# Smaller squares and stores in layer one, another schedule of weight decoding, and another buffer layout in layer two

## The chip, the cores and the metric

The kernel runs on one NeuronCore of a Trainium2 chip. Its five engines have queues of their own: PE multiplies matrices, DVE, ACT and POOL work on elements, and SP issues nearly all DMAs (transfers by the core's 16 DMA engines). The number compared is the device time of one execution in microseconds (us), the median of several.

## The reference

Float32 throughout, with 4 x 576 = 2304 tokens in 512 columns:

```python
x = attention(q, k, v, f)          # causal, with a decay per key; (4, 8, 576, 64) -> (2304, 512)
h = x @ moe_w_in                   # 512 x 2048
y = (h - np.tanh(h)) @ moe_w_out   # 2048 x 512
h = y @ moe2_w_in                  # layer one, below
r = np.maximum(h, 0.0)
out = (r * r) @ moe2_w_out         # layer two, below
```

## The kernel before

**Arithmetic.** Every float32 operand of a matmul is split into two parts, `hi` (written by ACT) and `lo` (the rest, by a subtraction on DVE), and a product is the sum of three matmul passes. The last two matrix products, here **layer one** and **layer two**, use Strassen and Winograd's scheme besides: a 2 x 2 block product is made of seven products instead of eight, numbered 1 to 7, from sums and differences of blocks.

**Stages.** Attention and the first MLP run first and interleaved, up to some 660 us. Then layer one: three blocks `i` of 768 tokens by eight column pairs `p` of the weights make 24 units `u`. A unit has seven products (`l1_product`) of six matmuls (128x128 weights, 384 tokens). The first four (6, 1, 7, 5) stand in the unit's own step, the others (2, 4, 3) in the next unit's, interleaved. `after1` evacuates each from PSUM: the sums go through `u2` into the four quarters of the unit's result, relu is taken on ACT, the square on POOL (`store1`), and SP stores the result to `gscr` in DRAM. Layer two has 36 groups `n` of seven products. `g_load` brings a group's four quarters from `gscr` into a buffer `graw` (SP), `g_sums` forms the differences (DVE), `g_split` makes the two parts in `gc` (ACT, then DVE), `l2_product` runs the matmuls, and `after2` and `store2` write the output.

**Weights.** `decode_w` turns the words of a weight matrix into float32: ACT (L193, L194), DVE (L200, L202), then the differences `wsum` on POOL (L246). Phase 1 are the eight column pairs of layer one: here (1,7) is the decode of pair 7. They are split at once (`split_all`, L302 and L303) into `ws` and `wq`. Phase 2 are the eight blocks of layer two; (2,k) is the decode of block k. These go to DRAM (`wscr`, L252 to L256), and `final_load` and `final_split` fetch and split them when layer one has done with the room. All decodes share two buffers "wide" (`wfull`, `wsum`), and one runs at a time: a decode asked for while another is at work waits in `pending` until `decoded()` is called. That happens in phase 1 behind the last split, and in phase 2 when the store of the sums has been issued. The words of block k + 1 are asked for (`load_w`) inside the decode of block k, and all the `wraw` of phase 2 share one buffer. A phase 2 decode is asked for at the start of unit 5 and of every second one behind it (`PRE`); phase 1 decodes come from `feed`, one per unit.

**Order.** A small clock in the code places the work: `cw.step` is one product, and `cw.later(k, fn)` runs `fn` k steps on. What is called in this sequence has its priority from it; a list scheduler then sets the order on each engine, and pools of buffers by `tag` set what must wait for what. `tc.high_priority` moves a piece of the program ahead in that ranking.

Of the kernel before, what the change touches and what calls it, by code (L numbers as in the profile page):

```python
# [10 lines left out]
F32 = mybir.dt.float32  # L11
# [9 lines left out]
P = 128  # L21
# [88 lines left out]
def fused_kernel(ctx: ExitStack, tc: tile.TileContext, q, k, v, f, w1i, w1o, w2i, w2o, out):  # L110
# [1057 lines left out]
    def after1(u, k, t):  # L1168
        i, p = units1[u]
        t3 = blocks3(t)  # L1170

        def add(o, a, b):
            nc.vector.tensor_tensor(o, in0=a, in1=b, op=ALU.add)  # L1173

        if k == 6:
# [5 lines left out]
        elif k == 1:  # L1181
            add(u2[u], t, u2[u])
        elif k == 7:
            gf[u, 1] = box2["m2"].tile([P, 3, 2, P], F32, tag="gt", name=f"g1_{u}", bufs=2)
            add(gf[u, 1][:, :, 1], t3, blocks3(u2[u]))
        elif k == 5:
            add(gf[u, 1][:, :, 1], t3, gf[u, 1][:, :, 1])
        elif k == 2:
            gf[u, 0] = m1.tile([P, 3, 2, P], F32, tag="x", name=f"g0_{u}", bufs=2)
            nc.scalar.activation(gf[u, 0][:, :, 0], t3, AF.Relu)  # L1190
        elif k == 4:
            g = gf[u, 1]
            add(g[:, :, 0], t3, blocks3(u2[u]))
            nc.scalar.activation(g, g, AF.Relu)  # L1194
            cw.later(1, lambda: store1(u, 1))
        else:
            g = gf[u, 0]
            add(g[:, :, 1], t3, blocks3(u2[u]))
            nc.scalar.activation(g[:, :, 1], g[:, :, 1], AF.Relu)
            cw.later(1, lambda: store1(u, 0))  # L1200

    def store1(u, fi):
        i, p = units1[u]
        g = gf.pop((u, fi))
# [260 lines left out]
```

## Time and profile before

| | us |
|---|---|
| median of three runs (lowest, highest) | 1063.67 (1059.83, 1066.32) |
| the profiled execution's own time | 1064.87 |
| its span in the profile | 1063.2 |

Times of the profile below count from the start of the span. The time of the execution is 1.7 us longer than the span, and 1.2 us above the median. TensorE's mean granted clock was 0.989 of its full speed. All engines have idle time, but PE little. What the page calls the idle time before an instruction, and names after an arrow, is the event that came last before it.

### The profile page before, as it was taken

What the parts mean: (1) busy time and instruction counts of PE and PEld (TensorE: products, weight loads), DVE (VectorE), ACT (ScalarE), POOL (GpSimd) and SP (SyncE); (2) the same over time, 40 slices, a digit from 0 to 9 for tenths busy, and PEclk for the clock granted to TensorE, in tenths of its full rate; (3) what the DMA queues carried; (4) which work ended last, traced back from release to release, by engine and by line L of the source; (5) the groups of instructions that cost most, each with busy time, mean ns of one, the idle gap of its engine ahead of it and who ended that gap; (6) DMA issues with size and microseconds to landing.
All of it is one profiled execution on the core that took longest, in us unless ns stands there. A gap on an engine that the chain in (4) does not pass through costs nothing.

```text
span 1063.2 us, 20566 instructions
## 1 busy us (share of the span) xinstructions
PE 1010.9 (95%) x7246; PEld 961.1 (90%) x7246; DVE 757.1 (71%) x1597; ACT 585.7 (55%) x1177; POOL 435.6 (41%) x576
## 2 busy tenths in 40 slices
PE   7989999999999999999999999988889869999998
PEld 5778899999999999999998878988888869999998
DVE  5897954777777767777756786577667788777775
ACT  5887854566766756766643574445355453333332
POOL 4663632455445555455502332666756340000000
PEclk9998999999999999999999999999999989999999
DMA  8937642333433333432231234657668853444442
GB/s 226 278 125 229 205 126 74 88 94 86 110 98 86 94 96 86 119 88 63 70 92 56 84 119 139 213 168 248 212 232 266 264 159 111 129 120 122 132 124 80
DMA packets 191335, 146.47 MB, mean 138 GB/s; under 512 B 83616, under 2 KB 168928, under 8 KB 191232
## 3 DMA queue, kind: packets, MB, share of 16 engines
q1 hardware_dynamic: 191184, 145.12, 46.1%
q8 instruction: 57, 0.93, 0.4%
q14 instruction: 46, 0.38, 0.1%
q10 hardware_dynamic: 48, 0.03, 0.0%
HBM read 100.47 MB, written 39.92 MB: 132 GB/s over the span
## 4 chain that ended last, share of the span: by engine, by line
PE 59%; DMA 7%; DVE 7%; issue 4%; POOL 4%; ACT 3%; SPq 2%; DVEq 0%; ACTq 0%; POOLq 0%
PE y L993 15%; PE h L953 15%; PE o L1302 13%; PE pt L737 4%; PE pv L808 3%; PE r L1161 3%; DMA wscr<-wfull 2%; POOL g L1205 2%; PE s L699 2%; PE s L700 2%; DVE gc L1289 1%; POOL wsum L246 1%; DMA gscr<-g 1%; DVE wfull L202 1%; DMA graw<-gscr 1%
## 5 line engine op out<-in xcount | busy, mean ns | idle before, releaser
L993 PE MATMUL y<-ghl,w 128*128 128x256 f32 (+1 forms) x1536 | 247.9, 304 | 2.9 <-DVE ghl L974 2.3
L993 PEld LDWEIGHTS y<-ghl,w 128*128 128x128 f32 x1536 | 211.5, 191 | 15.8 <-DVE ghl L974 3.6
L953 PE MATMUL h<-x,w 128*128 128x256 f32 x1344 | 199.6, 290 | 4.9 <-POOL w L218 3.8
L953 PEld LDWEIGHTS h<-x,w 128*128 128x128 f32 x1344 | 174.4, 190 | 9.7 <-POOL w L218 5.0
L1288 ACT ACTIVATE gc<-graw 128x1792 fp32r<-128x1792 f32 x36 | 60.6, 1699 | 112.9 <-DVE graw L1279 92.7
L1302 PE MATMUL o<-ws,gc 128*128 128x256 f32 x864 | 117.9, 287 | 0.0
L1161 PE MATMUL r<-yt,ws 128*128 128x384 f32 x576 | 109.5, 337 | 6.7 <-DVE g L1173 6.5
L1302 PEld LDWEIGHTS o<-ws,gc 128*128 128x128 f32 x864 | 111.2, 195 | 0.0
L1161 PEld LDWEIGHTS r<-yt,ws 128*128 128x128 f32 x576 | 99.8, 188 | 10.6 <-DVE g L1173 8.0
L530 POOL TENSOR_SCALAR Pb<-neg,ccol 128x384 f32<-128x384 f32 (+2 forms) x96 | 69.0, 718 | 91.4 <-PE pt L737 73.9
L644 ACT ACTIVATE Pb<-Pb,st 128x384 f32<-128x384 f32 (+2 forms) x96 | 67.6, 704 | 68.1 <-DVE st L635 67.8
L1302 PE MATMUL o<-wq,gc 128*128 128x256 f32 x648 | 92.8, 287 | 11.5 <-ACT gc L1288 7.3
L1205 POOL TENSOR_TENSOR g<-g 128x768 f32<-128x768 f32 x48 | 81.1, 1704 | 48.1 <-ACT g L1194 38.7
L658 POOL TENSOR_SCALAR Pb<-Pb,st 128x384 f32<-128x384 f32 (+2 forms) x96 | 67.0, 698 | 81.7 <-DVE st L654 50.9
L1302 PEld LDWEIGHTS o<-wq,gc 128*128 128x128 f32 x648 | 85.0, 194 | 12.8 <-ACT gc L1288 7.6
L1161 PE MATMUL r<-yt,wq 128*128 128x384 f32 x432 | 84.6, 337 | 11.5 <-ACT g L1190 6.2
L1161 PEld LDWEIGHTS r<-yt,wq 128*128 128x128 f32 x432 | 75.2, 188 | 14.8 <-ACT g L1190 7.5
L1289 DVE TENSOR_TENSOR gc<-graw,gc 128x1792 fp32r<-128x1792 f32 x36 | 73.2, 2054 | 15.8 <-ACT gc L1288 15.8
L635 DVE CUSTOM_DVE_ANT_0 Pb<-s,Pb 64x288 f32<-64x288 f32 (+2 forms) x160 | 73.8, 476 | 13.2 <-PE s L700 7.3
L966 DVE TENSOR_TENSOR g<-h,g 128x512 f32<-128x512 f32 x72 | 49.5, 687 | 31.1 <-ACT g L963 29.9
L246 POOL TENSOR_TENSOR wsum<-wfull 128x256 f32<-128x256 f32 x32 | 28.2, 882 | 84.1 <-DVE wfull L202 72.4
L743 DVE TENSOR_TENSOR PT<-pt,PT 128x384 fp32r<-128x384 f32 (+2 forms) x96 | 55.1, 574 | 10.3 <-ACT PT L742 5.6
(152 smaller groups left out, 1898.7 us busy)
## 6 DMA issues: line engine op xcount, KB each, us to landing
gscr<-g SPq DMA_DIRECT2D x48, 384.0 KB, 3.2
graw<-gscr SPq DMA_DIRECT2D x144, 128.0 KB, 2.6
wraw<-in_moe_w_in_dram SPq DMA_DIRECT2D x32, 512.0 KB, 4.7
wraw<-in_moe_w_out_dram SPq DMA_DIRECT2D x32, 512.0 KB, 5.3
neg<-cscr SPq DMA_DIRECT2D x32, 288.0 KB, 3.6
qk<-in_k_dram SPq DMA_DIRECT2D x48, 128.0 KB, 2.7
v<-in_v_dram SPq DMA_DIRECT2D x48, 128.0 KB, 2.7
wst<-wscr SPq DMA_DIRECT2D x6, 896.0 KB, 5.9
```

What stands on the lines that cost most here:

```text
L530: nc.gpsimd.tensor_scalar(pb[:rows, o : o + w], t[:rows, :w], ccol[:rows, ti, b * H + h : b * H + h + 1], 1.0, op0=ALU.add, op1=ALU.mult)
L635: nc.vector.tensor_tensor_reduce(out=d, in0=t[:rows, src : src + m], in1=d, scale=-0.125, scalar=3.0e38 if j == 0 else stat(0, x)[:rows], ...
L644: nc.scalar.activation(d, d, AF.Exp, bias=stat(len(parts) - 1, x)[:rows], scale=-1.0, accum_out=stat(2, x)[:rows])
L658: nc.gpsimd.tensor_scalar(d, d, r, 1.0, op0=ALU.mult, op1=ALU.mult)
L743: cw.later(LAG['trlo'], lambda: nc.vector.tensor_tensor(dst[1], src, dst[0].bitcast(F32), op=ALU.subtract))
L953: nc.tensor.matmul(o, lhsT=win(fc, wh, dc), rhs=xpart(j, dc, xh), start=dc == 0 and wh + xh == 0, stop=dc == ND - 1 and wh == 1)
L993: nc.tensor.matmul(o, lhsT=wout(fc, wh, i * P, P), rhs=ghl[:, xh, fj * n : fj * n + n], start=s == 0 and fj == 0 and wh + xh == 0 and i % ...
L1161: nc.tensor.matmul(t, lhsT=wprod(1, p, k, wh)[:, dc * P : (dc + 1) * P], rhs=yt[i, k][:, xh, dc], start=k in FIRST and dc == 0 and wh + xh ...
L1205: nc.gpsimd.tensor_tensor(g, in0=g, in1=g, op=ALU.mult)
L1288: nc.scalar.activation(c[:, 0], t[:, 1:8], AF.Copy)
L1289: nc.vector.tensor_tensor(c[:, 1], in0=t[:, 1:8], in1=c[:, 0].bitcast(F32), op=ALU.subtract)
L1302: nc.tensor.matmul(o, lhsT=gc[n][:, gh, GWHERE[k], e], rhs=wprod(2, 2 * q + e, k, wh), start=q == 0 and e == 0 and gh + wh == 0 and c0 == ...
```

## The change

**Layer one's results.** Before, a unit's result is kept in two tiles (`g0`, `g1`), each with two quarters, and squared and stored as such. In the changed kernel the lower two quarters are tiles apart: quarter (1,1), complete after product 5, has relu, square and store at once, and lies in a tile that two units share; quarter (1,0), complete after product 4, has a buffer of its own in tag "g". The upper two remain one tile. So there are three squares and three stores in a unit instead of two, and `gscr` has another layout.

**Decoding.** The phase 2 decodes are asked for at product numbers (`PREDECODE`; a unit has seven) instead of every second unit, the first words are loaded at step 0, and the first decode is asked for at product 11.

**Layer two.** Inputs `graw` have four buffers (two of room freed by weights, two in `gx`) where only the first two groups had buffers of their own and the others shared two. At the boundary `gc` of group 0 is placed and split first. The staging of weight blocks 5, 6 and 7 changes places, and block 7 is loaded at the boundary.

```diff
@@ final_load
-        if p == NP2 - 1:
+        if p == NP2 - 3:
             s_, r = wide(f"wst_s{p}", F32), wide(f"wst_r{p}", F32)[:, :768]
...
+        elif p == NP2 - 1:
+            s_ = m1.tile([P, 1024], F32, tag="ghl", name=f"wst_s{p}", bufs=2)
+            r = m1.tile([P, 768], F32, tag="ghl", name=f"wst_r{p}", bufs=2)
+            parts = [(s_, 0, 4), (r, 4, 7)]
...
-    gscr = [dram.tile([P, 3, NF, NB], F32, name=f"gscr_{i}") for i in range(3)]
+    gscr = [dram.tile([P, NF, 2, 3, P], F32, name=f"gscr_{i}") for i in range(3)]
@@ after1
         elif k == 7:
-            gf[u, 1] = box2["m2"].tile([P, 3, 2, P], F32, tag="gt", name=f"g1_{u}", bufs=2)
-            add(gf[u, 1][:, :, 1], t3, blocks3(u2[u]))
+            if u % 2 == 0:
+                gf[u] = box2["m2"].tile([P, 2, NU1], F32, tag="gt", name=f"g11_{u}", bufs=2)
+            gf[u, 1, 1] = gf[u - u % 2][:, u % 2]
+            add(gf[u, 1, 1], t, u2[u])
         elif k == 5:
-            add(gf[u, 1][:, :, 1], t3, gf[u, 1][:, :, 1])
+            g = gf[u, 1, 1]
+            add(g, t, g)
+            relu(g, g)
+            cw.later(1, lambda: store1(u, gf.pop((u, 1, 1)), gscr[i][:, 2 * p + 1, 1]))
...
         elif k == 4:
-            g = gf[u, 1]
-            add(g[:, :, 0], t3, blocks3(u2[u]))
-            nc.scalar.activation(g, g, AF.Relu)
-            cw.later(1, lambda: store1(u, 1))
+            g = m1.tile([P, NU1], F32, tag="g", name=f"g10_{u}", bufs=3)
+            add(g, t, u2[u])
+            relu(g, g)
+            cw.later(1, lambda: store1(u, g, gscr[i][:, 2 * p + 1, 0]))
...
@@ layer1
-            if s >= PRE and (s - PRE) % 2 == 0 and (s - PRE) // 2 < NP2:
-                decode_w(2, (s - PRE) // 2)
-            if s == PRE - 1:
+            if s == 0:
                 load_w(2, 0)
...
-            for x in (todo if s else []):
+            for at, x in (enumerate(todo, 7 * s) if s else []):
+                if at in PREDECODE:
+                    decode_w(2, PREDECODE.index(at))
                 cw.step(lambda: l1_product(*x))
...
-    PRE = 5
-    FREED = (1, 2, 3, 4, 5, 6, None, 6)
+    FREED = (1, 2, 3, 4, 5, 6, None, None)
+    PREDECODE = (11, 23, 35, 47, 61, 73, 86, 120)
@@ g_tile, g_load
-        if n < 2:
-            t = wp.tile([P, 8, 2, P], F32, tag=f"w{15 - n}", name=f"graw_{n}", bufs=1)
+        if n % 4 < 2:
+            t = wp.tile([P, 8, 2, P], F32, tag=f"w{15 - n % 4}", name=f"graw_{n}", bufs=1)
         else:
             t = box2["m3"].tile([P, 8, 2, P], F32, tag="gx", name=f"graw_{n}", bufs=2)
...
@@ layer2
-        for x in range(2):
-            g_tile(2 + x)
-        with tc.high_priority(offset=L2HOT):
-            final_load(NP2 - 2)
-        box2["m3"].tile([P, 256], F32, tag="pad", name="pad", bufs=1)
-        for n in (2, 0, 1):
-            gc_tile(n)
+        gc_tile(0)
         with tc.high_priority(offset=L2HOT):
             g_split(0)
+            final_load(NP2 - 2)
+        box2["m3"].tile([P, 768], F32, tag="pad", name="pad", bufs=1)
+        for n in (2, 1):
+            gc_tile(n)
         with tc.high_priority(offset=L2HOT // 2):
+            g_split(1)
             for n in (2, 3):
                 g_load(n)
-            g_split(1)
-        cw.later(2, lambda: final_split(NP2 - 2))
+        final_load(NP2 - 1)
+        final_split(NP2 - 3)
+        cw.later(4, lambda: final_split(NP2 - 2))
         cw.later(9, lambda: final_split(NP2 - 1))
```

Three places show the order that results, the second on two engines. A row has its line, the operation, and the output, then the inputs; the last number of a name is a running one. The first place is SP's queue at the start of layer one, where the last pieces of y go to `yscr`, and `wraw_2_0` is loaded for the decode (2,0). Before:

```order
L1006 DMA yscr_7_84<-ys_7_0_8563 128x256
L1006 DMA yscr_8_85<-ys_7_0_8563 128x256
L1006 DMA yscr_7_84<-ys_7_1_8570 128x256
...
L1006 DMA yscr_8_85<-ys_7_2_8577 128x256
L139 DMA wraw_2_0_8787<-in_moe2_w_out_dram 128x1024
L1006 DMA yscr_7_84<-ys_7_3_8584 128x256
L1006 DMA yscr_8_85<-ys_7_3_8584 128x256
L139 DMA wraw_2_0_8787<-in_moe2_w_out_dram 128x1024
L1206 DMA gscr_0_122<-g1_0_8546 384x1x256
```

Changed:

```order
L1010 DMA yscr_7_84<-ys_7_0_8566 128x256
L1214 DMA gscr_0_122<-g11_0_8546 128x384
L1010 DMA yscr_8_85<-ys_7_0_8566 128x256
L1010 DMA yscr_7_84<-ys_7_1_8573 128x256
...
L1010 DMA yscr_8_85<-ys_7_2_8580 128x256
L139 DMA wraw_2_0_8594<-in_moe2_w_out_dram 128x1024
L1010 DMA yscr_7_84<-ys_7_3_8587 128x256
L1010 DMA yscr_8_85<-ys_7_3_8587 128x256
L139 DMA wraw_2_0_8594<-in_moe2_w_out_dram 128x1024
```

The store of the half result of unit 0 (`g11_0`) now stands behind the first store of y; the first store of a result stood behind both loads of `wraw_2_0`.

The second place is the decode (1,7) on ACT (`wfull_1_7`, then `wraw_1_7`, L193 and L194; the split into `wq` is L302), in the midst of relus and copies (`g0`, `g10`, `spare`). Before:

```order
L194 ACTIVATE wraw_2_0_8787<-wraw_2_0_8787 128x512
...
L1180 ACTIVATE spare_8518<-r6_3_8726 128x384
L193 ACTIVATE wfull_1_7_8978<-wraw_1_7_8588 128x512
L194 ACTIVATE wfull_1_7_8978<-wraw_1_7_8588 128x512
L1190 ACTIVATE g0_2_8751<-r1_2_8675 128x3x128
L193 ACTIVATE wraw_1_7_8588<-wraw_1_7_8588 128x512
L194 ACTIVATE wraw_1_7_8588<-wraw_1_7_8588 128x512
L1194 ACTIVATE g1_2_8699<-g1_2_8699 128x768
L302 ACTIVATE wq_1_1_2_8533<-wfull_1_7_8978 128x512
```

Changed:

```order
L193 ACTIVATE wfull_2_1_8777<-wraw_2_1_8700 128x512
L194 ACTIVATE wfull_2_1_8777<-wraw_2_1_8700 128x512
...
L193 ACTIVATE wfull_2_2_8911<-wraw_2_2_8828 128x512
L194 ACTIVATE wfull_2_2_8911<-wraw_2_2_8828 128x512
...
L1183 ACTIVATE spare_8518<-r6_6_8992 128x384
L1176 ACTIVATE g0_5_9020<-r1_5_8924 128x384
L193 ACTIVATE wfull_1_7_9038<-wraw_1_7_8591 128x512
L194 ACTIVATE wfull_1_7_9038<-wraw_1_7_8591 128x512
L1176 ACTIVATE g10_5_9041<-g10_5_9041 128x384
L193 ACTIVATE wraw_1_7_8591<-wraw_1_7_8591 128x512
...
L302 ACTIVATE wq_1_1_2_8533<-wfull_1_7_9038 128x512
```

(1,7) stood behind `wraw_2_0`, the last row of the decode (2,0), and between copies for units 3 and 2; now (2,1) and (2,2) stand ahead of it, and the copy for unit 6.

The products that need these weights are those of unit 7 on PE (`r6_7`, `r1_7` and so on; the name has the product, then the unit). Before:

```order
L1161 MATMUL r5_6_8983<-yt_0_5_8322,ws_1_6_8532 128x384 x6
L1161 MATMUL r5_5_8911<-yt_0_3_8468,ws_1_5_8440 128x384 x6
L1161 MATMUL r6_7_9026<-yt_0_6_8169,ws_1_7_9014 128x384 x6
L1161 MATMUL r1_7_9037<-yt_0_1_8224,wq_1_1_2_8533 128x384 x6
L1161 MATMUL r1_6_8945<-yt_0_2_8371,wq_1_1_1_8441 128x384 x6
L1161 MATMUL r7_7_9060<-yt_0_7_8272,ws_1_7_9014 128x384 x6
L1161 MATMUL r7_6_8962<-yt_0_4_8419,wq_1_1_2_8533 128x384 x6
L1161 MATMUL r5_7_9085<-yt_0_5_8322,ws_1_7_9014 128x384 x6
L1161 MATMUL r5_6_8983<-yt_0_3_8468,ws_1_6_8532 128x384 x6
```

Changed:

```order
L1162 MATMUL r5_6_9044<-yt_0_5_8322,ws_1_6_8532 128x384 x6
L1162 MATMUL r5_5_8968<-yt_0_3_8468,ws_1_5_8440 128x384 x6
L1162 MATMUL r1_6_9004<-yt_0_2_8371,wq_1_1_1_8441 128x384 x6
L1162 MATMUL r7_6_9022<-yt_0_4_8419,wq_1_1_2_8533 128x384 x6
L1162 MATMUL r5_6_9044<-yt_0_3_8468,ws_1_6_8532 128x384 x6
L1162 MATMUL r6_7_9090<-yt_0_6_8169,ws_1_7_9078 128x384 x2
L1162 MATMUL r1_7_9101<-yt_0_1_8224,wq_1_1_2_8533 128x384 x3
L1162 MATMUL r6_7_9090<-yt_0_6_8169,ws_1_7_9078 128x384 x4
L1162 MATMUL r1_7_9101<-yt_0_1_8224,wq_1_1_2_8533 128x384 x3
```

Unit 7's first product stood third here and now stands sixth, behind the last three products of unit 6 (`r1_6`, `r7_6`, `r5_6`: products 2, 4 and 3, each added to the bank of an earlier one); its first two products are drawn into one another.

The third place is DVE at the boundary between the layers, where `g1_23`, `g10_23` and `g0_23` are the last results of layer one, and `gc_0` the first input of layer two. Before:

```order
L1173 TENSOR_TENSOR g1_23_10305<-r7_23_10298,u2_23_10277 128x3x128
L303 TENSOR_TENSOR wq_2_1_2_10422<-wst_r7_10260,wq_2_1_2_10422 128x512
L1173 TENSOR_TENSOR g0_23_10349<-r5_23_10315,u2_23_10277 128x3x128
L303 TENSOR_TENSOR wq_2_1_2_10422<-wst_r7_10260,wq_2_1_2_10422 128x256
L303 TENSOR_TENSOR ws_2_7_10483<-wst_s7_10259,ws_2_7_10483 128x1024
L1289 TENSOR_TENSOR gc_0_10388<-graw_0_10106,gc_0_10388 128x1792
L1289 TENSOR_TENSOR gc_1_10389<-graw_1_10111,gc_1_10389 128x1792
L1276 TENSOR_TENSOR graw_2_10378<-graw_2_10378 128x256
```

Changed:

```order
L1173 TENSOR_TENSOR g10_23_10432<-r7_23_10376,u2_23_10354 128x384
L1173 TENSOR_TENSOR g0_23_10423<-r5_23_10393,u2_23_10354 128x384
L1297 TENSOR_TENSOR gc_0_10452<-graw_0_10178,gc_0_10452 128x1792
L1297 TENSOR_TENSOR gc_1_10463<-graw_1_10183,gc_1_10463 128x1792
L1284 TENSOR_TENSOR graw_2_10466<-graw_2_10466 128x256
L303 TENSOR_TENSOR ws_2_6_10526<-wst_0_6_10455,ws_2_6_10526 128x512
L1285 TENSOR_TENSOR graw_2_10466<-graw_2_10466 128x512
L303 TENSOR_TENSOR ws_2_6_10526<-wst_2_6_10456,ws_2_6_10526 128x512
L1287 TENSOR_TENSOR graw_2_10466<-graw_2_10466 128x256
```

The splits of weight blocks 6 and 7 (`ws_2_6`, `ws_2_7` and their `wq`) stood ahead of `gc_0`; now they stand behind `gc_1`.

## Rows read from the trace of the kernel before

**Rows 1.** The page: busy time and its share of the span, by engine.

```profile
PE 1010.9 (95%) x7246; PEld 961.1 (90%) x7246; DVE 757.1 (71%) x1597; ACT 585.7 (55%) x1177; POOL 435.6 (41%) x576
```

**Rows 2.** Timeline of PE: start, duration (us), group; in brackets idle time and releaser.

```profile
665.83 1.23 PE L1161 MATMUL r<-yt,ws 128*128 128x384 f32 x6
...
715.53 2.36 PE L1161 MATMUL r<-yt,wq 128*128 128x384 f32 x12 [2.24 <-ACT g L1190]
...
718.77 1.20 PE L1161 MATMUL r<-yt,wq 128*128 128x384 f32 x6
719.81 3.28 PE L1161 MATMUL r<-yt,ws 128*128 128x384 f32 x18
...
859.72 1.21 PE L1161 MATMUL r<-yt,ws 128*128 128x384 f32 x6
868.20 0.79 PE L1302 MATMUL o<-wq,gc 128*128 128x256 f32 x2 [7.27 <-ACT gc L1288]
...
871.39 1.01 PE L1302 MATMUL o<-wq,gc 128*128 128x256 f32 x3 [1.11 <-DVE gc L1289]
```

**Rows 3.** Windows: length, busy PE, PEld, DVE, ACT, POOL, clock, DMA share, GB/s.

```profile
705.00:720.00 15.00, 12.76 (x73) 12.21 (x73) 7.21 (x14) 6.87 (x12) 8.95 (x11) 1.00 0.80 256
868.00:880.00 12.00, 10.69 (x66) 10.39 (x67) 9.88 (x12) 5.31 (x6) 1.45 (x1) 0.70 0.63 186
880.00:900.00 20.00, 20.00 (x169) 20.00 (x169) 16.29 (x24) 7.45 (x6) 0.00 (x0) 1.00 0.44 132
980.00:1000.00 20.00, 18.16 (x139) 17.95 (x138) 15.14 (x21) 7.28 (x5) 0.00 (x0) 0.91 0.43 129
```

**Rows 4.** Waits of PE from 655 us to 1064: total us, times, longest.

```profile
PE r L1161 <- DVE g L1173: 7.5, 8, 1.5
PE o L1302 <- ACT gc L1288: 7.3, 1, 7.3
PE r L1161 <- ACT g L1190: 6.2, 4, 2.2
PE o L1302 <- DVE gc L1289: 4.3, 4, 1.8
PE r L1161 <- DVE yt L1106: 3.7, 4, 1.3
```

**Rows 5.** Waits of all engines, 655 to 870 us.

```profile
DVE g L1173 <- DMA gscr<-g: 22.8, 11, 3.8
...
ACT wfull L193 <- DMA wscr<-wfull: 11.2, 3, 4.3
```

**Rows 6.** Timeline of POOL.

```profile
668.17 1.86 POOL L1117 TENSOR_TENSOR yr<-yr 128x768 f32<-128x768 f32 x1
...
674.23 1.47 POOL L1205 TENSOR_TENSOR g<-g 128x768 f32<-128x768 f32 x1 [2.40 <-ACT g L1194]
676.33 0.74 POOL L246 TENSOR_TENSOR wsum<-wfull 128x256 f32<-128x256 f32 x1 [0.63 <-DVE wfull L202]
```

**Rows 7.** Timeline of SP's queue.

```profile
667.93 0.33 SPq L139 DMA_DIRECT2D wraw<-in_moe_w_out_dram  x1
...
679.71 1.10 SPq L139 DMA_DIRECT2D wraw<-in_moe_w_out_dram  x2
```

**Rows 8.** Timeline of ACT, the first instruction of four decodes: (2,0), (1,7), (2,1), (2,2).

```profile
672.21 0.66 ACT L193 ACTIVATE wfull<-wraw 128x512 uint32<-128x512 uint32 x1 [2.54 <-DMA wraw<-in_moe_w_out_dram]
...
686.59 0.66 ACT L193 ACTIVATE wfull<-wraw 128x512 uint32<-128x512 uint32 x1 [4.30 <-DMA wscr<-wfull]
...
696.53 0.64 ACT L193 ACTIVATE wfull<-wraw 128x512 uint32<-128x512 uint32 x1
...
712.64 0.66 ACT L193 ACTIVATE wfull<-wraw 128x512 uint32<-128x512 uint32 x1 [3.04 <-DMA wscr<-wfull]
```

**Rows 9.** Timeline of DVE at the boundary.

```profile
866.18 1.95 DVE L303 TENSOR_TENSOR ws<-wst_s,ws 128x1024 fp32r<-128x1024 f32 x1 [0.46 <-ACT ws L302]
868.18 5.09 DVE L1289 TENSOR_TENSOR gc<-graw,gc 128x1792 fp32r<-128x1792 f32 x2
```

More of the change, by code (lines that the diff above doesn't have):

```diff
@@ L1146, in spare @@
         return spares[0]
-    def blocks3(x):
-        return x.rearrange("p (b n) -> p b n", b=3)
     def l1_product(u, k):
@@ L1169, in after1, with relu @@
         i, p = units1[u]
-        t3 = blocks3(t)
         def add(o, a, b):
             nc.vector.tensor_tensor(o, in0=a, in1=b, op=ALU.add)
+        def relu(o, a):
+            nc.scalar.activation(o, a, AF.Relu)
         if k == 6:
@@ L1183, in after1, with store1 @@
         elif k == 7:
-            gf[u, 1] = box2["m2"].tile([P, 3, 2, P], F32, tag="gt", name=f"g1_{u}", bufs=2)
-            add(gf[u, 1][:, :, 1], t3, blocks3(u2[u]))
+            if u % 2 == 0:
+                gf[u] = box2["m2"].tile([P, 2, NU1], F32, tag="gt", name=f"g11_{u}", bufs=2)
+            gf[u, 1, 1] = gf[u - u % 2][:, u % 2]
+            add(gf[u, 1, 1], t, u2[u])
         elif k == 5:
-            add(gf[u, 1][:, :, 1], t3, gf[u, 1][:, :, 1])
+            g = gf[u, 1, 1]
+            add(g, t, g)
+            relu(g, g)
+            cw.later(1, lambda: store1(u, gf.pop((u, 1, 1)), gscr[i][:, 2 * p + 1, 1]))
         elif k == 2:
-            gf[u, 0] = m1.tile([P, 3, 2, P], F32, tag="x", name=f"g0_{u}", bufs=2)
-            nc.scalar.activation(gf[u, 0][:, :, 0], t3, AF.Relu)
+            gf[u, 0] = m1.tile([P, 2, NU1], F32, tag="x", name=f"g0_{u}", bufs=2)
+            relu(gf[u, 0][:, 0], t)
         elif k == 4:
-            g = gf[u, 1]
-            add(g[:, :, 0], t3, blocks3(u2[u]))
-            nc.scalar.activation(g, g, AF.Relu)
-            cw.later(1, lambda: store1(u, 1))
-        else:
[L1197 to L1204, printed above, removed]
+            g = m1.tile([P, NU1], F32, tag="g", name=f"g10_{u}", bufs=3)
+            add(g, t, u2[u])
+            relu(g, g)
+            cw.later(1, lambda: store1(u, g, gscr[i][:, 2 * p + 1, 0]))
+        else:
+            g = gf.pop((u, 0))
+            add(g[:, 1], t, u2[u])
+            relu(g[:, 1], g[:, 1])
+            cw.later(1, lambda: store1(u, g.rearrange("p h n -> p (h n)"),
+                                       gscr[i][:, 2 * p].rearrange("p h b n -> p (h b n)")))
+    def store1(u, g, dst):
         nc.gpsimd.tensor_tensor(g, in0=g, in1=g, op=ALU.mult)
-        cw.later(2, lambda: nc.sync.dma_start(gscr[i][:, :, 2 * p + fi], g.rearrange("p b t n -> p b (t n)")))
+        src = g if len(dst.shape) == 2 else g.rearrange("p (b n) -> p b n", b=3)
+        cw.later(2, lambda: nc.sync.dma_start(dst, src))
     def layer1():
@@ L1245, in layer1 @@
                     final_load(p)
-                if s == last + FREED[p] + 1 and p < NP2 - 2:
+                if s == last + FREED[p] + 1 and p < NP2 - 3:
                     final_split(p)
-    PRE = 5
-    FREED = (1, 2, 3, 4, 5, 6, None, 6)
+    FREED = (1, 2, 3, 4, 5, 6, None, None)
+    PREDECODE = (11, 23, 35, 47, 61, 73, 86, 120)
     AT2 = {1: (0, 0), 6: (0, 256), 7: (1, 0), 2: (1, 256), 5: (2, 0), 4: (2, 256), 3: (3, 0)}
@@ L1267, in g_load @@
         t = graws[n] if n in graws else g_tile(n)
-        src = gscr[j // 3][:, j % 3, 4 * q : 4 * q + 4].rearrange("p (e i) (h t) -> p i h e t", i=2, h=2)
         for slot, h, i in ((0, 1, 0), (5, 0, 0), (7, 1, 1), (6, 0, 1)):
-            nc.sync.dma_start(t[:, slot], src[:, i, h])
+            src = gscr[j // 3][:, 4 * q : 4 * q + 4, h, j % 3].rearrange("p (e i) t -> p i e t", i=2)
+            nc.sync.dma_start(t[:, slot], src[:, i])
     def g_sums(n):
```

## Prediction

> **What bounds the kernel now.** I read the page's busy line first (PE 95% [rows 1]), then the timeline of PE, the windows around its stops and the table of its waits, and only then the engines that the waits name. The end of the run is set by PE from 665.83 us on: layer one runs one product (six matmuls) every 1.04 us when nothing is late (from 718.77 to 719.81 [rows 2]), and layer two one matmul every 20 / 169 = 0.118 us (the stretch 880 to 900 [rows 3]). From 665.83 us, the first product of unit 1, to 859.72 + 1.21 = 860.93 us, the end of layer one, 164 products take 195.1 us; undisturbed they would take 170.6. So layer one loses 24.5 us. The gap to layer two takes 7.27 us and a second wait of 1.11 us behind it [rows 2]. In 868 to 880 us only 66 matmuls end, where 12 / 0.118 = 102 could: 4.3 us lost, of which the first 0.2 us and the 1.11 us are idle; the other 3 us are the clock, granted at 0.70 as a mean of the stretch, while a wait of 2.24 us in 705 to 720 left it at 1.00 [rows 2, 3]. In 980 to 1000 us 139 matmuls end instead of 169: 3.5 us, idle and clock together. PE's own table splits the waits: on DVE and ACT evacuating PSUM in layer one 7.5 + 6.2, on the split of the next inputs 3.7, at and behind the boundary 7.3 + 4.3 [rows 4]. At most some 24.5 + 11.6 + 5 = 41 us can be had without touching PE's work.
>
> **The change, part by part.**
>
> *Squares and stores by half tiles.* DVE waits 22.8 us in 11 places for a store of layer one to land, since its two buffers come free late [rows 5]. The new buffers are held for more units, so I take all these waits away. But PE has other banks to write meanwhile, and the evacuation waits it shows add up to 13.7 us over both engines [rows 4], and the longest of them, 2.24 us on ACT [rows 2], ends behind a block of ACT that a decode made, not a store (below). I give this part 2 us; its ends are 0 and 7.5 (all of PE's waits on DVE in layer one). The squares grow from 48 to 72 instructions on POOL with the same elements: 256 columns take 0.74 us and 768 take 1.47 [rows 6], so 384 take about 0.92 (an estimate on that line), and two halves 0.37 us more than one whole, 24 x 0.37 = 9 us on POOL, hidden, since it is busy 41% of the span [rows 1]. ACT gets 24 more instructions and SP 24 more stores at some 0.55 us (two issues take 1.10) [rows 7], 13 us, hidden too, save in one place.
>
> *That place.* The order shows the first half store of unit 0 on SP before seven stores of y and both loads of wraw_2_0. The square it waits for stands on POOL behind two subtractions; it takes the place of the third, which starts at 668.17 us [rows 6]. So it ends at about 669.1, and SP, which issued the first load of wraw_2_0 at 667.93 [rows 7], comes to it after that store and five more, 6 x 0.5 later: about 672.0. The decode of (2,0) waits for this load; it began at 672.21 [rows 8] and I move it by 4 us to 676.2.
>
> *Decoding placed by product.* The order places (2,0) where it stood, but (1,7), the weights of layer one's unit 7, moves behind (2,1) and (2,2). Each decode of layer two keeps its buffer until its stores have landed; the next one's first instruction on ACT waits for that (11.2 us in three places [rows 5]). The distance from one such start to the next is 14.4 us (672.21 to 686.59) and 16.1 us (696.53 to 712.64), and 9.9 us behind (1,7), which stores nothing (686.59 to 696.53) [rows 8]. Before, (1,7) stood second in this chain. Now it stands fourth: three distances lie ahead of it. I take 14.0 each, a little under the shortest one seen with a store, because the split of (1,7) no longer stands on DVE between them; the ends are 9.9 and 16.1. So (1,7) starts at 676.2 + 42 = 718.2, and its products can start 9.5 us later (it took 9.9 to the next decode): 727.7. Unit 7 began at about 712.1 (its first product ends where the wait of 2.24 begins, at 715.53 - 2.24 = 713.29) [rows 2]. The scheduler has drawn three products of unit 6 ahead of it, so by 727.7 us PE has done 45 products, 46.8 us of work from 665.83: 15.1 us are lost by then, of which about 10 us in one idle stretch. Behind so long a stretch the clock falls, as after the 7.27 us: 3 us more (ends: 0, and 6 if both stretches' cost comes). Of the 24.5 us, before had lost 2.6 us by 712.1 (42 products are 43.7 us), 21.9 behind it. Of these I strike 10: about 2.5 us that follow from ACT's block at 712.64 [rows 8] (its wait of 2.24 us [rows 2] and a little), which now lies ahead of unit 7, the 2 us of the stores, and 5.5 us because PE comes later, so that the decodes that follow are in time, and because (2,7) no longer falls into the split of the third block's inputs. 12 stay (ends: 7 and 19). Layer one: 15.1 + 3 + 12 - 24.5 = +5.6 us.
>
> [...] The row shows 0.70 behind 7.27 us of idling and 1.00 in the stretch that holds a wait of 2.24 us. [...]
>
> *Buffer layout at the boundary.* DVE split the last two weight blocks (to 868.1 us, the last piece 1.95 us) before it could split layer two's first inputs, at 868.18, 5.09 us for two [rows 9]. Now the first inputs come first, and these weights follow. The split on ACT can start when the last but one product is evacuated, about at the end T of layer one, and so PE's first passes soon behind it instead of at T + 7.3 [rows 2]; DVE's part takes some 2.5 us more (half of 5.09). PE loses about 4 us there instead of 8.6 (0.2 + 7.27 + 1.11), but then the two weight blocks, loaded only at the boundary, come late for the fourth group of inputs; I charge 2 us. Clock: up to the 3 us less, of which I take 2.4. Together -4.6 + 2 - 2.4 = -5 (ends: -9 and 0).
>
> *Four input buffers.* Loads of inputs can start two groups earlier. The waits behind 900 us, and the clock after them, are 3.5 + 1.1 + 0.3 = about 5 us (4.3 - 1.1 of waits [rows 4], the rest clock [rows 3]). DVE is at 15.14 of 20 us in 980 to 1000 [rows 3] and a split is some 2.5 us of its time (5.09 for two [rows 9]), so a little stays: -4.5 (ends: -5 and 0).
>
> Sum on the profiled execution: 1064.9 + 5.6 - 5 - 4.5 = 1061.0; that execution stands 1.2 us above the median of the runs (1063.67), which leaves 1059.8. Both ends of the strike list lean towards less, so I take 1059.
>
> **The rivals.**
>
> *The decode chain keeps up.* If the distances are as short as the one without a store, 9.9 us, unit 7 starts at 676.2 + 29.7 + 9.5 = 715.4: no idle stretch, no clock, 2.8 us lost by then instead of 15.1 + 3. That gives 1059 - 15.3 = 1044. For it: the one distance of 9.9 is a decode followed by a free buffer, and of the new order's decodes only the waits for the stores, 3.0 to 4.3 us each [rows 8], make the others longer. Against it: no distance with a store was below 14.4.
>
> *The chain at its slowest, slower than before.* Place: first product of unit 7. At 16.1 us each and 9.9 to the products it starts at 676.2 + 48.3 + 9.9 = 734.4, 6.7 us later than in the sum, and with PE so late the splits of the next block fall on it at once: of the 21.9 us, 17 stay and not 12. 1059 + 6.7 + 5 = 1071. Each us at this place is one us at the end; from 732.4 on (1064 - 1059 = 5 us later) the change loses. For it: the later of the two distances with a store is the longer one, and it lies where the chain's end lies now.
>
> *The change does not do what it says.* The order shows that the scheduler puts (2,0) at the same place for program positions 35 and 11 (in products). If the chain of stores alone sets all starts, the new numbers do nothing but swap (1,7), and if the inputs of layer two are bound by the splits and not the loads, the buffers do nothing either: 1064.
>
> **How the numbers follow.** Runs of this kernel spread by 0.6%, so 1% (1053 to 1074) is about what tells a change from none. The forecast 1059 (1053 to 1066) gets 0.43, the chain that keeps up (1040 to 1052) 0.34, the slow chain (1066 to 1080) 0.17, nothing done 0.06. Faster by over 1% is the second: 0.36 with the edge of the first. Slower by over 1% is the upper part of the slow chain: 0.14. The range leaves out 1 in 10 at each end: 1043 to 1071.
>
> **What the changed profile would show.** An idle stretch of PE, 7 to 12 us long, before the first product of unit 7, near 718 to 728 us, ended by ACT's or DVE's split of ws, with a granted clock under 0.9 behind it; ACT idle for wscr<-wfull before that; DVE's waits on gscr<-g gone; SP silent near 665 to 669 us; the gap before layer two below 3 us; no wait of PE on gc behind 900 us. I am wrong if PE goes through unit 7 without a stop of over 4 us (then near 1045), or if the weights (2,6) and (2,7) stop layer two for long (then above 1065).

## The result and the profile after

The changed kernel takes 1053.21 us (median of five runs, 1051.69 to 1055.44), the kernel before 1063.67 (now of five, too, with the same ends); the ratio is 0.9906, 95% interval 0.9878 to 0.9934. The forecast was 1059, the range 1043 to 1071. So the time lies in the range, at the lower edge of the forecast class (1053 to 1066), but the gain is 10.5 us where 4.7 were forecast, more than twice as much. The profiled execution took 1052.08 us, its span 1050.4.

The busy line of the page of the changed kernel, against [rows 1]:

```profile
PE 1010.5 (96%) x7246; PEld 965.3 (92%) x7246; DVE 742.7 (71%) x1597; ACT 589.9 (56%) x1201; POOL 440.7 (42%) x600
```

PE does the same work in a shorter span; with 24 more instructions on each, the busy time of ACT grows by 4 us and that of POOL by 5.

PE's timeline in the changed kernel, against [rows 2]:

```profile
666.74 1.23 PE L1162 MATMUL r<-yt,ws 128*128 128x384 f32 x6
...
716.74 1.32 PE L1162 MATMUL r<-yt,ws 128*128 128x384 f32 x6 [1.50 <-DVE g L1173]
723.99 1.01 PE L1162 MATMUL r<-yt,ws 128*128 128x384 f32 x2 [5.93 <-ACT ws L302]
...
728.00 3.81 PE L1162 MATMUL r<-yt,ws 128*128 128x384 f32 x18
...
764.78 4.21 PE L1162 MATMUL r<-yt,wq 128*128 128x384 f32 x12 [3.85 <-ACT g L1176]
...
857.85 1.21 PE L1162 MATMUL r<-yt,ws 128*128 128x384 f32 x6
860.80 0.51 PE L1310 MATMUL o<-wq,gc 128*128 128x256 f32 x2 [1.75 <-ACT gc L1296]
```

Read as before: layer one now lasts from 666.74 to 859.06, 192.3 us instead of 195.1; the gap is 1.74 us instead of 7.27; layer two, from 860.80 to the end of the span, takes 189.6 us instead of 195.0. With a start that is 0.9 us later the sum is 0.9 - 2.8 - 5.5 - 5.4 = -12.8 us, the difference of the spans.

PE's waits from 640 us on, against [rows 4]:

```profile
PE r L1162 <- ACT ws L302: 5.9, 1, 5.9
PE r L1162 <- ACT g L1176: 5.1, 2, 3.9
PE r L1162 <- DVE g L1173: 2.1, 2, 1.5
PE o L1310 <- ACT gc L1296: 1.7, 1, 1.7
PE r L1162 <- DVE yt L1110: 0.9, 1, 0.9
PE o L1310 <- DVE gc L1297: 0.8, 1, 0.8
```

A new wait of 5.9 us on the split of weights stands where 7.5 us on DVE's evacuations have fallen to 2.1. The row of DVE's 22.8 us of waits for stores [rows 5] is gone from its table; 8.1 us in two places, before an instruction of a decode (L200), are still put down to a store.

Windows of the changed kernel, columns as in [rows 3]:

```profile
705.00:745.00 40.00, 32.57 (x174) 31.92 (x173) 30.88 (x46) 23.68 (x45) 24.55 (x24) 0.87 0.52 184
...
990.00:1010.00 20.00, 20.00 (x169) 20.00 (x168) 14.64 (x24) 7.29 (x5) 0.00 (x0) 1.00 0.43 124
```

The clock of 0.87 belongs to the stop before unit 7 (granted at 0.50 from 724 to 728 us); behind 900 us PE's table has no wait.

The four decodes on ACT, against [rows 8], now in the order (2,0), (2,1), (2,2), (1,7):

```profile
676.92 0.66 ACT L193 ACTIVATE wfull<-wraw 128x512 uint32<-128x512 uint32 x1 [3.83 <-DMA wraw<-in_moe_w_out_dram]
...
690.00 0.67 ACT L193 ACTIVATE wfull<-wraw 128x512 uint32<-128x512 uint32 x1 [3.29 <-DMA wscr<-wfull]
...
703.34 0.67 ACT L193 ACTIVATE wfull<-wraw 128x512 uint32<-128x512 uint32 x1 [3.55 <-DMA wscr<-wfull]
...
714.23 0.66 ACT L193 ACTIVATE wfull<-wraw 128x512 uint32<-128x512 uint32 x1 [3.36 <-DMA wscr<-wfull]
```

And SP's queue at the place of [rows 7]:

```profile
665.59 0.33 SPq L1010 DMA_DIRECT2D yscr<-ys  x1
669.78 0.33 SPq L1214 DMA_DIRECT2D gscr<-g  x1
670.16 2.57 SPq L1010 DMA_DIRECT2D yscr<-ys  x5
672.83 0.38 SPq L139 DMA_DIRECT2D wraw<-in_moe_w_out_dram  x1
```

The square of that half, in POOL's timeline:

```profile
668.93 0.82 POOL L1212 TENSOR_TENSOR g<-g 128x384 f32<-128x384 f32 x1
```

SP issues nothing for 3.9 us (665.92 to 669.78) because the half store waits for its square, which ends at 669.75, and the load of `wraw_2_0` follows at 672.83, 4.9 us later than before.

### The profile page after: what moved, and what is told of

It reads as the page before. It is cut to its first block, busy times and chain, and to the rows that moved or that the text cites. A ratio compares the mean times of both kernels' runs of the same rounds, so it can differ in the third digit from the quotient of the medians.

```text
span 1050.4 us, 20663 instructions
## 1 busy us (share of the span) xinstructions
PE 1010.5 (96%) x7246; PEld 965.3 (92%) x7246; DVE 742.7 (71%) x1597; ACT 589.9 (56%) x1201; POOL 440.7 (42%) x600
## 4 chain that ended last, share of the span: by engine, by line
PE 70%; DMA 5%; DVE 4%; issue 3%; POOL 3%; ACT 2%; SPq 0%; DVEq 0%; POOLq 0%; ACTq 0%
PE o L1310 17%; PE y L997 15%; PE h L957 15%; PE r L1162 9%; PE pt L741 4%; PE pv L812 3%; PE s L703 2%; PE s L704 2%; POOL g L1212 1%; POOL wsum L246 1%; DMA K<-K 1%; DMA yr<-yscr 1%; DMA gscr<-g 1%; DMA wscr<-wfull 1%; DVE wfull L202 1%
## 5 line engine op out<-in xcount | busy, mean ns | idle before, releaser
L1162 PEld LDWEIGHTS r<-yt,ws 128*128 128x128 f32 x576 | 102.4, 192 | 10.4 <-ACT ws L302 6.3
L1212 POOL TENSOR_TENSOR g<-g 128x384 f32<-128x384 f32 (+1 forms) x72 | 86.3, 1211 | 56.6 <-ACT g L1176 45.3
L1162 PEld LDWEIGHTS r<-yt,wq 128*128 128x128 f32 x432 | 78.1, 194 | 7.0 <-ACT g L1176 5.7
L1176 ACT ACTIVATE g<-g 128x384 f32<-128x384 f32 x72 | 36.7, 521 | 50.9 <-DVE g L1173 50.7
```

The lines of the kernel that those rows point to most:

```text
L1162: nc.tensor.matmul(t, lhsT=wprod(1, p, k, wh)[:, dc * P : (dc + 1) * P], rhs=yt[i, k][:, xh, dc], start=k in FIRST and dc == 0 and wh + xh ...
```

## The experiments

There are four series, the first with the changed kernel alone, each with 5 to 20 runs of the kernel before on the same chip (its medians: 1063.67, 1067.96, 1066.32 and 1067.91 us) and 4 to 11 runs of each other kernel. So ratios are compared across series, and times inside one. The last three columns are read from each profile as above: layer one from unit 1's first product, the gap, layer two to the end of the span.

| kernel | ratio to before | 95% interval | layer one | gap | layer two |
|---|---|---|---|---|---|
| before | 1 | | 195.1 | 7.3 | 195.0 |
| changed | 0.9906 | 0.9878 to 0.9934 | 192.3 | 1.7 | 189.6 |
| changed, third series | 0.9876 | 0.9837 to 0.9915 | 197.2 | 1.7 | 188.3 |
| decodes at the old places | 0.9956 | 0.9942 to 0.9970 | 204.7 | 1.8 | 189.3 |
| first half store late | 0.9823 | 0.9807 to 0.9838 | 189.5 | 1.7 | 188.0 |
| two input buffers | 0.9958 | 0.9941 to 0.9974 | 195.5 | 1.8 | 198.3 |
| old code at the boundary | 0.9837 | 0.9814 to 0.9861 | 192.5 | 2.0 | 187.6 |
| the same again | 0.9851 | 0.9828 to 0.9873 | 193.9 | 2.0 | 188.1 |
| whole stores | 0.9963 | 0.9938 to 0.9988 | 197.5 | 9.7 | 188.6 |
| (1,7) first | 0.9880 | 0.9833 to 0.9926 | 196.1 | 1.7 | 188.3 |
| three edits together | 0.9866 | 0.9826 to 0.9906 | 189.9 | 2.0 | 189.2 |
| before, late staging | 1.0019 | 1.0003 to 1.0036 | 193.7 | 3.7 | 203.1 |
| boundary and buffers alone | 0.9976 | 0.9952 to 1.0000 | 199.9 | 8.8 | 187.9 |
| late store, old boundary | 0.9827 | 0.9806 to 0.9848 | 190.3 | 2.0 | 187.6 |

The two rows of the changed kernel differ by 5 us in layer one: one profile tells no difference of a few us there, and layer one starts anywhere from 663.6 to 672.8 us in these profiles.

### Decodes at the old places

```diff
-    PREDECODE = (11, 23, 35, 47, 61, 73, 86, 120)
+    PREDECODE = (35, 49, 63, 77, 91, 105, 119, 133)
```

The first words are still loaded at step 0.

> The changed kernel with the decodes of layer two asked for at products 35, 49, ..., 133 again, which puts (1,7) second in the chain. My theory: the stop of 5.93 us before unit 7 and the slow clock behind it (some 2.6 us) go, and part of what was lost later comes back: 1046 us (1043 to 1050), first product of unit 7 at about 711, no stop of PE over 3 us there. Rival, the new places are what shortened the rest of layer one: the waits behind unit 7 come back in full, 1053 to 1060.

The ratio is 0.9956, 0.5 to 0.8% or 5 to 9 us above the two of the changed kernel. The stop before unit 7 is gone (its largest near there is 1.47 us), as my theory had it, but layer one takes 204.7 us: the rival is right in the time. The waits from 640 us on (PE) and from 660 to 870 (ACT):

```profile
PE r L1162 <- ACT g L1176: 13.5, 6, 3.8
PE r L1162 <- DVE g L1173: 7.3, 5, 4.1
...
ACT wfull L193 <- DMA wscr<-wfull: 27.1, 5, 7.6
```

In the changed kernel the last row is

```profile
ACT wfull L193 <- DMA wscr<-wfull: 14.5, 5, 3.5
```

ACT stands 27.1 us for the stores of an earlier decode to land instead of 14.5, or 18.1 in the second profile of the changed kernel. What stands behind the waiting decode in ACT's queue are relus and copies out of PSUM, and PE waits for these.

### The first half store late

```diff
@@ after1, k == 5
-            cw.later(1, lambda: store1(u, gf.pop((u, 1, 1)), gscr[i][:, 2 * p + 1, 1]))
+            go = lambda: store1(u, gf.pop((u, 1, 1)), gscr[i][:, 2 * p + 1, 1])
+            if u == 0:
+                held.append(go)
+            else:
+                cw.later(1, go)
@@ layer1
+                if at == 10:
+                    cw.later(1, held.pop())
```

> The changed kernel with unit 0's first half store (and its square) moved behind both loads of wraw_2_0 on SP. My theory: SP no longer waits 3.9 us there, (2,0) starts at about 673 instead of 676.9, all four decodes of the chain move by 3.9 us, the stop before unit 7 shrinks from 5.93 to about 2 us and the clock stays up: 1047 to 1049. Rival: the loads or POOL set the chain, nothing moves: 1053.

The ratio is 0.9823: 6 to 9 us less than the changed kernel, more than the 4 to 6 expected. In the timelines of ACT (decode (2,0)) and PE:

```profile
672.25 0.68 ACT L193 ACTIVATE wfull<-wraw 128x512 uint32<-128x512 uint32 x1 [2.25 <-DMA wraw<-in_moe_w_out_dram]
...
720.37 1.01 PE L1162 MATMUL r<-yt,ws 128*128 128x384 f32 x2 [5.93 <-ACT ws L302]
```

(2,0) starts 4.7 us earlier and unit 7 3.6; 0.6 us of each is an earlier start of layer one in this profile. So SP's wait does move the decode by the 4 us that the prediction gave it. But the stop itself is as long as it was, not some 2 us as my theory had it: PE, too, comes earlier, since evacuations that it waits for ahead of the stop stand behind the same decodes (its wait of 1.25 us for ACT at 691.64 us in the changed kernel is gone).

### Two input buffers

```diff
-        if n % 4 < 2:
-            t = wp.tile([P, 8, 2, P], F32, tag=f"w{15 - n % 4}", name=f"graw_{n}", bufs=1)
+        if n < 2:
+            t = wp.tile([P, 8, 2, P], F32, tag=f"w{15 - n}", name=f"graw_{n}", bufs=1)
```

> The changed kernel with two buffers for inputs of layer two instead of four (the first two groups as they are). My theory: the waits of PE for gc behind 900 us come back with their clock, 3 to 5 us: 1057. Rival: the waits went with the order at the boundary, and the buffers do nothing: 1053.

0.9958, so 5 to 9 us above the changed kernel; layer two grows from 189.6 to 198.3 us, and PE's waits for inputs come back, first those of its matmuls from 640 us on, then those of its weight loads (PEld) from 880 us on:

```profile
PE o L1310 <- DVE gc L1297: 3.2, 7, 0.8
...
PEld o L1310 <- DVE gc L1297: 6.8, 18, 1.0
```

In the changed kernel these are 0.8 us in one place and nothing. The theory is right on the waits and too small in the time; the clock is not part of it (1.00 from 900 to 1020 us). The buffers matter more here than the kernel before showed; my reading, which no run tests, is that with the gap closed layer two starts sooner and the loads can't follow.

### The old code at the boundary, twice

```diff
@@ layer2
-        gc_tile(0)
+        for x in range(2):
+            g_tile(2 + x)
         with tc.high_priority(offset=L2HOT):
-            g_split(0)
             final_load(NP2 - 2)
-        box2["m3"].tile([P, 768], F32, tag="pad", name="pad", bufs=1)
-        for n in (2, 1):
+        box2["m3"].tile([P, 256], F32, tag="pad", name="pad", bufs=1)
+        for n in (2, 0, 1):
             gc_tile(n)
...
```

The staging in `final_load` and the rest of the start of `layer2` are the first version's, too.

> The changed kernel with the staging of blocks 5 to 7 and the start of layer two as before, four input buffers kept. My theory: the gap before layer two is 7 us again instead of 1.7, with some 1 us of clock: 1059 to 1060. Rival: the gap was due to late results of layer one, not to the splits that stood ahead: 1053 to 1055.

> The run with the first code at the boundary once more. If that code is better by itself: ratio to the kernel before 0.984 again. Rival, the first ratio was chance or the chip's: 0.988 to 0.990, as the changed kernel has.

0.9837 and 0.9851, with a gap of 2.0 us. My theory falls: this code does not close the gap. The rival, by which nothing would be lost, is nearer, but its reason was another (below). By the ratios the old code is even 3 to 7 us faster; as some of the intervals overlap, whether it is faster at all stays open.

### The changed kernel again, and whole stores

> The changed kernel itself, beside the others on the same chip. Both theories: ratio to the kernel before 0.9906 as measured first, within 0.3%. The runs below are read as differences from this one.

0.9876, 0.3% lower, and the two intervals overlap.

The next kernel, of the same series, has the old `after1`, `store1`, `gscr` and `g_load`:

```diff
-            g = m1.tile([P, NU1], F32, tag="g", name=f"g10_{u}", bufs=3)
-            add(g, t, u2[u])
-            relu(g, g)
-            cw.later(1, lambda: store1(u, g, gscr[i][:, 2 * p + 1, 0]))
+            g = gf[u, 1]
+            add(g[:, :, 0], t3, blocks3(u2[u]))
+            nc.scalar.activation(g, g, AF.Relu)
+            cw.later(1, lambda: store1(u, 1))
...
```

> The changed kernel with squares and stores of the first form (two tiles in a unit, first gscr layout). Theory formed after the first runs: the half tile in tag g is what keeps the staging of weight block 6 from being loaded before the end of layer one; without it the splits of blocks 6 and 7 stand ahead of gc_0 on DVE again, and the gap before layer two is 6 to 8 us instead of 1.7, in spite of the new code at the boundary; SP's wait for the first half store goes (as in the run with the late store: 5 us less); stores cost PE some 2 us in layer one. Sum: 1 to 5 us above the control. Rival, as I predicted: the layout at the boundary alone closes the gap, which stays below 3 us, and the time is 2 us less to 2 us more than the control's.

1063.17 us, 9.6 above the control (the changed kernel of that series). The gap is 9.73 us, longer than before the change, though all the new code at the boundary is in. PE's first product of layer two, then DVE's last work ahead of it:

```profile
875.03 0.80 PE L1306 MATMUL o<-wq,gc 128*128 128x256 f32 x2 [9.73 <-ACT gc L1292]
...
864.01 3.46 DVE L303 TENSOR_TENSOR ws<-wst,ws 128x512 fp32r<-128x512 f32 x2 [0.51 <-ACT ws L302]
...
871.23 1.69 DVE L303 TENSOR_TENSOR ws<-wst_s,ws 128x1024 fp32r<-128x1024 f32 x1 [2.82 <-ACT ws L302]
...
875.01 3.96 DVE L1293 TENSOR_TENSOR gc<-graw,gc 128x1792 fp32r<-128x1792 f32 x2 [0.87 <-ACT gc L1292]
```

The splits of weight blocks 6 and 7 are ahead of `gc` again. In the changed kernel DVE's rows at this place are

```profile
860.78 3.96 DVE L1297 TENSOR_TENSOR gc<-graw,gc 128x1792 fp32r<-128x1792 f32 x2 [1.08 <-ACT gc L1296]
...
866.28 0.69 DVE L303 TENSOR_TENSOR ws<-wst,ws 128x512 fp32r<-128x512 f32 x1
```

Block 6 is staged in tag "g". With half tiles, layer one's results hold that tag to the end, so the load, and the split behind it, can only come late; block 7's follows. SP's timeline shows it: the two loads of 256 KB into that tag are issued at 790.04 and 792.23 us with whole stores, and at the boundary in the changed kernel (first row: with whole stores, the earlier of the two; second row: changed, both):

```profile
790.04 0.33 SPq L333 DMA_DIRECT2D wst<-wscr  x1
...
858.09 0.87 SPq L333 DMA_DIRECT2D wst<-wscr  x2
```

With the old code at the boundary and half tiles both are issued at 860.71 us. That is what took the splits out of the way.

The theory is right on this and wrong in its sum of 1 to 5 us: the 5 us that SP's wait was to give are not there. The wait is gone, and (2,0) starts 6.2 us behind unit 1's first product instead of the control's 10.1, but the three distances of the chain behind it are 14.2, 14.2 and 12.2 us, and PE stops for 7.4 us before unit 7.

### (1,7) first, and three edits together

```diff
@@ layer1
-                    feed.upto(NF + p + 1)
+                    feed.upto(NF + (NP2 if s else 1))
```

> The changed kernel with all decodes of phase 1 asked for at unit 1, which puts (1,7) ahead of (2,0) in the chain; the places of layer two's decodes stay. My theory: the stop of PE before unit 7 (5.93 us, with the 1.5 us before it and the slow clock behind, some 9 us in all) goes, the new places keep what they give behind unit 7, and (2,0) starts no later, since its words arrive at 677 anyway: 7 to 10 us less than the control. Rival: the stop only moves, since every decode of layer two is one decode later in the chain, and evacuations that stand behind its waits on ACT stop PE elsewhere: 3 us less to 3 us more than the control.

1055.73 us beside 1053.57: no gain, the rival. PE stops no longer for weights, but ACT's waits for stores grow to 27.8 us from 18.1, and PE waits 5.9 us for inputs of layer one instead of 1.1; its waits for evacuations stay at 10 us. In the timeline of ACT two decodes of layer two, (2,2) and (2,3):

```profile
711.12 0.66 ACT L193 ACTIVATE wfull<-wraw 128x512 uint32<-128x512 uint32 x1 [6.08 <-DMA wscr<-wfull]
...
727.18 0.66 ACT L193 ACTIVATE wfull<-wraw 128x512 uint32<-128x512 uint32 x1 [6.21 <-DMA wscr<-wfull]
```

> Three edits on the changed kernel: (1,7) ahead of (2,0), unit 0's first half store behind the loads of wraw_2_0, and the first code at the boundary. If the parts add up, as my theory has it: 7 to 10 us from the first, 0 to 5 from the second (less than the 9 measured alone, as the stop before unit 7 is gone), 2 from the third (layer two took 187.6 us with it instead of 189.6): 9 to 15 us less than the control. Rival, the parts share one cause (the chain starts earlier): no more than the best of them alone, 9 us.

This kernel has that edit, the late store and the old boundary. 1053.17 us: the parts don't add up. ACT's waits for stores are 27.3 us here, too, and yet layer one is down to 189.9 us, with PE waiting 2.0 us for ACT's evacuations (13.5 with the old places). So the sum of ACT's waits is no price by itself; it depends on what stands behind them. Layer one starts late, at

```profile
672.83 1.33 PE L1158 MATMUL r<-yt,ws 128*128 128x384 f32 x6 [0.75 <-DVE ys L1003]
```

where the control began at 668.48. Of these 4.4 us, 3.4 are there already at unit 0's first product (664.97 against 661.53), ahead of unit 1, where the program asks for the decodes; the rest is the wait in this row.

### The kernel before with late staging

```diff
@@ final_load
-            s_, r = wide(f"wst_s{p}", F32), wide(f"wst_r{p}", F32)[:, :768]
-            parts = [(s_, 0, 4), (r, 4, 7)]
+            parts = [(m1.tile([P, 512], F32, tag="x", name=f"wst_{x}_{p}", bufs=2), x, x + 2) for x in (0, 2)]
+            parts.append((wide(f"wst_r{p}", F32)[:, :768], 4, 7))
         elif p == NP2 - 2:
-            parts = [(m1.tile([P, 512], F32, tag="g", name=f"wst_{x}_{p}", bufs=3), x, x + 2) for x in (0, 2)]
+            parts = [(m1.tile([P, 512], F32, tag="x", name=f"wst_{x}_{p}", bufs=2), x, x + 2) for x in (0, 2)]
@@
-    FREED = (1, 2, 3, 4, 5, 6, None, 6)
+    FREED = (1, 2, 3, 4, 5, 6, None, None)
@@ layer2
             final_load(NP2 - 2)
+            final_load(NP2 - 1)
```

> The kernel before with one thing changed: the staging of weight blocks 6 and 7 is put into tag x, whose buffers layer one's results hold to the end, and block 7 is loaded at the boundary. Theory: this alone moves the splits of these blocks behind gc_0 and gc_1 on DVE, the gap before layer two falls from 7.3 us to 2 or 3, and the time by 4 to 6 us. Rival: what is moved comes back as waits for weights in the first groups of layer two, 2 us either way.

The ratio is 1.0019: no gain. PE's start of layer two and its waits there:

```profile
865.65 0.80 PE L1302 MATMUL o<-wq,gc 128*128 128x256 f32 x2 [3.73 <-ACT gc L1288]
```

```profile
PE o L1302 <- DVE gc L1289: 9.0, 9, 1.7
PE o L1302 <- ACT gc L1288: 5.0, 2, 3.7
```

The gap is halved by the tags alone (the theory had it at 2 to 3 us), but the time is 2 us longer, not 4 to 6 shorter. Layer two takes 203.1 us instead of 195.0: what was won comes back, and more, and PE's table shows waits for inputs (9.0 us for DVE instead of 4.3), none for weights as the rival had it.

### Boundary and buffers alone; late store with the old boundary

The first has the edits of the whole stores and of the old places together.

> The changed kernel with squares and stores and with the places of decodes as before: what is left is the code at the boundary and the four input buffers. Theory: the buffers give 4 to 6 us behind 900 us, the gap before layer two stays at 7 to 10 us, in all 2 to 5 us below the kernel before. Rival, as I predicted for these two parts: 9.5 us below it, with a gap under 3 us.

0.9976, in the theory's range, with a gap of 8.8 us; the 9.5 us that I predicted for these two parts are not there.

> The changed kernel with two edits: unit 0's first half store behind the loads of wraw_2_0, and the first code at the boundary. If they add up (5 and 3.5 us in the runs apart): 1045 us. Rival, no more than the late store alone: 1048.

1049.33 us (1048.08 to 1051.38) beside 1052.45 (1051.24 to 1053.12) for the old boundary alone: the late store gives 3 us there. The two edits don't add up: 0.9827 is the late store's own 0.9823. These two have the lowest ratios measured. Both are faster than the kernel before; their intervals lie below that of the changed kernel's first series and just touch that of its second measurement.

## Why the prediction came out as it did

**The place on SP: right.** The store held SP 3.9 us; (2,0) began at 676.92, predicted 676.2, and putting the store later brought 3 us in one pair of kernels and 6 to 9, across series, in the other.

**The chain of decodes and the stop: right mechanism, too large a term.** The step that failed is "14.0 each" for the three distances. They were 13.1, 13.3 and 10.9 us, so (1,7) began at 714.23 instead of 718.2. With whole stores they are 14.2, 14.2 and 12.2 (one profile), so the shorter distances seem to come with the half tiles, whose effect on the chain I left out; how is open. The 9.5 us from there to the product held (9.8). By 723.99 us PE had lost 57.25 - 46.8 = 10.5 us, not 15.1. The clock behind the stop cost 2.5 us, not 3: 12 matmuls from 723.99 to 728.00 took 4.0 us instead of 2.1, and the next 18 took 3.6 instead of 3.1, with the clock granted at 0.50 and then 0.85. The stop was 5.93 us, and so missed the sign that I gave for it, 7 to 12 us.

**The rest of layer one: too large.** Of 192.3 - 170.6 = 21.7 us lost in all, 21.7 - 10.5 - 2.5 = 8.7 come behind unit 7's start; 12 were predicted. 6.4 of the 8.7 are one stop, 3.85 us at 764.78, with the clock behind it (granted at 0.50 from 764.78 to 768.80 us): 12 matmuls took 4.0 us instead of 2.1, the next 6 took 1.6 instead of 1.0, together 2.5. The three terms make the 8.4 us between +5.6 and -2.8. That I took the new places for a loss alone is an error behind it: with half tiles the old places are 0.5 to 0.8% slower, though there PE has no long stop before unit 7. That ACT's waits are the reason is argued, not shown. That an idle stretch costs more than its length held here (2.5 us on 5.93, 2.5 on 3.85), but not with one price: 5.93 us cost 1.6 more in the kernel with the late store.

**The boundary: the sum right, the cause wrong.** The gap shrank by 5.5 us. I gave this to the code at the boundary; that code alone leaves 8.8 us and without it 2.0 remain. The half tiles in tag "g" did it, the part for which I allowed 2 us, in layer one. The clock, which I had 2.4 us better, is what it was: in the first 10 us of layer two 51 matmuls end, at 0.66, in the changed kernel (row in the last section) as in the kernel before (columns as in [rows 3]):

```profile
868.20:878.20 10.00, 8.88 (x51) 8.59 (x52) 8.26 (x9) 3.31 (x4) 1.25 (x1) 0.66 0.76 223
```

So it is luck that this term came out.

**Four buffers: right.** The waits behind 900 us went, and layer two lost 5.4 us of its length, where 4.5 were predicted; without the buffers the run is 5 to 9 us longer.

**The parts are not a sum.** With four buffers and the new boundary, half tiles alone (old places) stand at 0.9956, new places alone (whole stores) at 0.9963, neither at 0.9976, both at 0.9906 and 0.9876. Each alone gives next to nothing: half tiles close the gap (7 us), but with the old places lose most of it again, in layer one by the profiles (204.7 us instead of 199.9, one profile each). The longer waits of ACT in that case are shown; why they lengthen is not, nor that they alone make layer one longer, since they are as long in the kernel with the three edits. A third "wide" buffer, which would have told, was not tried.

## What to carry to other kernels

A buffer's tag also sets when a later load can start (here 790.04 or 858.09 us), and so what a scheduler puts ahead of the critical work: look for the gap's cause in who held the buffer, not only in the code at the gap. Price a gap together with the stage behind it: with two input buffers in that stage, what the smaller gap gave (3.5 us) was lost there again (8.1 us). A stop of PE that hangs on a chain of decodes shared with the evacuations moves when the order does; starting the chain earlier (here by one store moved on SP) is what paid, with half tiles.

## What the runs showed of the hardware

**The clock after the same idle time.** PE was busy 18 of the 18 us that end 2 us ahead of layer two in three profiles, and then idle for 1.75 and 0.84 us in each. The first 10 us of layer two, in the changed kernel, in its second profile and in that with the late store (columns as in [rows 3]):

```profile
860.80:870.80 10.00, 9.16 (x51) 8.95 (x52) 8.80 (x11) 6.69 (x8) 3.18 (x1) 0.66 1.04 328
```

```profile
867.40:877.40 10.00, 9.15 (x62) 8.95 (x63) 8.79 (x11) 6.70 (x8) 3.19 (x1) 0.83 1.03 328
```

```profile
857.38:867.38 10.00, 9.16 (x74) 8.96 (x75) 9.02 (x11) 6.59 (x8) 3.18 (x1) 1.00 1.05 336
```

51, 62 or 74 matmuls, the first two in the same kernel: the same idle cost up to 23 x 0.118 = 2.7 us or nothing. So a difference of 2 us in layer two can be the clock's alone: at the same 0.83 in these 10 us the old (second profile) and the new code at the boundary take 188.1 and 188.3 us. What makes the clock vary behind the same idle time, these rows don't show.

**DVE beside POOL.** In the changed kernel the same decode instruction on DVE, with POOL's row beside the second:

```profile
756.34 0.69 DVE L200 SCALAR_TENSOR_TENSOR wfull<-wfull 128x512 uint32<-128x512 uint32 x1 [3.09 <-DMA yr<-yscr]
...
758.19 2.33 DVE L200 SCALAR_TENSOR_TENSOR wraw<-wraw 128x512 uint32<-128x512 uint32 x1
```

```profile
757.83 2.15 POOL L1121 TENSOR_TENSOR spare<-yr,yr 128x768 f32<-128x768 f32 x1
759.93 1.91 POOL L1212 TENSOR_TENSOR g<-g 128x768 f32<-128x768 f32 x1
```

0.69 us became 2.33 under POOL's subtraction and square, just ahead of the stop of 3.85 us at 764.78. From 640 to 800 us, the five instructions of this line that took over 0.9 us (0.98 to 2.33) lie beside POOL's work for most of their length (0.8 us at least); the others, 0.68 or 0.69, for at most 0.48 us. No run here takes POOL's work away, so that this work is the cause is argued, not shown.
